# Computing K of four token tiles from raw x at the start, and centring and scaling the kept result later

## The chip, the cores and the metric

The kernel runs on one core of one Trainium2 chip. The metric is the device time of one execution in microseconds (us), the median of several runs; lower is better. Before the change three runs gave 209.97, 210.48 and 213.08 us, median 210.48.

The core has five engines, each with its own instruction stream, synchronised by semaphores: PE (TensorE, matrix multiplication into PSUM), DVE (VectorE), ACT (ScalarE), POOL (GpSimd) and SP (SyncE, which here only issues DMAs). PSUM has 8 banks of 128 x 512 fp32. A DMA is issued by SP or ACT, each of which has a queue of its own, and is carried by 16 DMA engines that both queues share.

## The reference, cut to what matters

`x` is 2048 tokens by D = 640 in bf16. The output is x + A(LN(x)) + B(LN(x)), where LN subtracts the mean of each token and divides by its standard deviation, without learned weights.

```python
def _A_ref(x, wqkv, wo):                 # linear attention, H = 32 heads of 20
    qkv = (x @ wqkv) ...                 # D x 3D: q, k, v
    phi = lambda t: jnp.where(t > 0, t + 1, jnp.exp(t)) + 1e-6
    pq, pk = phi(q), phi(k)
    kv = jnp.einsum("bhsd,bhse->bhde", pk, v)
    z = jnp.einsum("bhsd->bhd", pk)
    num = jnp.einsum("bhqd,bhde->bhqe", pq, kv)
    den = jnp.einsum("bhqd,bhd->bhq", pq, z)[..., None] + 1e-6
    o = num / den
    return ... o ... @ wo
def _B_ref(x, w1, b1, w2, b2):           # dense layer, hidden size F = 1536
    h = _gelu(x @ w1 + b1)
    return h @ w2 + b2
xn = _layernorm(x)
return x + _A_ref(xn, A_wqkv, A_wo) + _B_ref(xn, B_w1, B_b1, B_w2, B_b2)
```

## The kernel before

The 2048 tokens are 16 tiles of P = 128. D is DT = 5 blocks of 128, F is JT = 12 blocks. Everything stays in SBUF: `x_in` (token-major x, later overwritten by `PK` = phi(K)), `xn_tm` (token-major normalised x), `xnT` (feature-major normalised x), `HG` (the gelu output, feature-major), `PQ` (phi(Q), feature-major) and the weights. Every instruction stream is written out by hand: `Pl.ins(engine, ...)` appends to that engine's list, in program order, and adds the waits that its reads and writes need. So an instruction that waits holds up all that stands behind it on its engine, and a DMA that waits on SP holds up the DMAs behind it. PSUM banks are handed out in a ring by `take`.

The stages, in the order of PE:

1. Opening. SP loads x tile by tile, and the four column pieces of W1 between them (`dma_x`, L228; `dma_w1`, L239; piece 0 goes on ACT's queue). PE runs ten filler matmuls on zeros (`filler`, L296). For each tile DVE computes statistics in two halves (`ln_half`, L309, `bn_stats`) and aggregates them (`ln_aggr`, L317), POOL raises the variance to -0.5 (`pow`), and DVE normalises (`ln_norm`, L330). `ln_next(t)` (L422) issues the statistics of tile t + 1, then the normalisation of tile t, then the aggregation of t + 1, in this order on DVE. Tiles 0 to 3 are transposed on PE against an identity matrix and copied from PSUM to `xnT` by DVE or ACT (`transp0`, `transp`, `xnT_copy`); tiles 4 to 15 are transposed by DMA out of `xn_tm` (`dma_start_transpose`, L447, on SP).
2. H. A unit (`h_unit`, L351) is one block of F for n token tiles: five matmuls of n x 128 columns into one bank, and one gelu on ACT from there into `HG`. `units(t0, n, lo, hi)` runs units lo to hi - 1. The first units, for tiles 0 and 1, run as each piece of W1 arrives: 36 units with n = 1, then 30 with n = 2 and 24 with n = 4 (some of n = 2 among the first).
3. K (L471). For each of 16 tiles ten matmuls of 320 columns into a pair of banks; `phi` (L455) is one exp on ACT, one min/add on DVE and one max/add on DVE that reads PSUM and writes `PK` over `x_in`. The K columns of Wqkv are loaded on SP after the DMA transposes.
4. G (L508). For each of five blocks f: 16 tiles times two matmuls accumulate xn^T PK; ACT copies the pair of banks out. Meanwhile DVE sums PK over the tiles in fp32 (`token_sum`, L497) and splits the sum into two bf16 parts (`zhl`); ahead of the last block, PE multiplies them by ones (`z_step`, L486).
5. Q, the small products for the value side (`kvt_step`, `m_step`), the denominators, and the output stage (W2 products and PQ times M into the same banks, 15 tiles and a last one in three parts).

Of the kernel before, what the change touches and what calls it, by code (L numbers as in the profile page):

```python
# [112 lines left out]
def bass_parallel_sum__linear_attn_block__dense_activation_gelu__prompt_kernel(  # L113
# [4 lines left out]
    NT = S // P  # L118
# [18 lines left out]
    with contextlib.ExitStack() as es:  # L137
# [21 lines left out]
        zhl = Mf[:, 2 * D:4 * D].rearrange("p (a d) -> p a d", a=2)  # L159
        b1tmp = sb("b1tmp", [JT, P], BF16)  # L160
# [40 lines left out]
        r_x = [R_("x%d" % t) for t in range(NT)]  # L201
        r_xr = [R_("xr%d" % c) for c in range(NC)]
# [5 lines left out]
        r_Wq, r_Wk, r_Wv, r_W2, r_Wo = R_("Wq"), R_("Wk"), R_("Wv"), R_("W2"), R_("Wo")  # L208
        r_b1tmp, r_b1c, r_b2 = R_("b1tmp"), R_("b1c"), R_("b2")
        r_ident, r_small, r_masks, r_bmask, r_E4, r_warm = R_("ident"), R_("small"), R_("masks"), R_("bmask"), R_("E4"), R_("warm")  # L210
        r_stats = [[R_("stats%d_%d" % (i, h)) for h in range(2)] for i in range(4)]
        r_aggr = [R_("aggr%d" % i) for i in range(4)]
        r_rstd = [R_("rstd%d" % i) for i in range(4)]
# [7 lines left out]
        r_zsum, r_zhl, r_z, r_ZB = R_("zsum"), R_("zhl"), R_("z"), R_("ZB")  # L221
# [11 lines left out]
        def dma_w(eng, dst, src, res):  # L233
            Pl.ins(eng, lambda e: e.dma_start(dst, src), writes=[res], dma=True)  # L234
# [4 lines left out]
        def dma_w1(i, eng="sync"):  # L239
            dma_w(eng, W1[:, :, i * FW:(i + 1) * FW], w1v[:, :, i * FW:(i + 1) * FW], r_W1[i])  # L240
        dma_x(0, 1)
        dma_w("scalar", b1tmp[:], B_b1.rearrange("(a p) -> a p", p=P), r_b1tmp)
        dma_w1(0, "scalar")
        dma_x(1, 1)
        dma_w1(1)
        dma_x(2, 1)
        dma_w1(2)
        dma_x(3, 1)
        dma_w1(3)
        dma_x(4, 2)  # L250
        dma_x(6, 2)
        for c in range(2, NC):
            dma_x(c * CH, CH)
        x_done = len(Pl.records["sync"])
        dma_w("sync", Wqkv[:, :, D:2 * D], wqv[:, :, D:2 * D], r_Wk)
# [10 lines left out]
        Pl.ins(g, lambda e: e.memset(onesb[:], 1.0), writes=[r_small])  # L266
        Pl.ins(g, lambda e: e.memset(ident[:], 0.0), writes=[r_ident])
# [40 lines left out]

        def ln_half(t, h):  # L309
            s = t % 4  # L310
            Pl.ins(v, lambda e: e.bn_stats(stats[:, s, 6 * h:6 * h + 6], x_in[:, t, h * HW:(h + 1) * HW]),  # L311
                   reads=[r_x[t]], writes=[r_stats[s][h]])
            if h == 0:
                Pl.ins(g, lambda e: e.tensor_single_scalar(stats[:, s, 2:3], stats[:, s, 2:3], D * EPS, ALU.add),
                       reads=[r_stats[s][0]], writes=[r_stats[s][0]])

        def ln_aggr(t):  # L317
            s = t % 4
# [11 lines left out]
        def ln_norm(t):  # L330
            s = t % 4
# [32 lines left out]
        CA = 2 * P  # L364
        r_xnA, r_xnB = R_("xn0A"), R_("xn0B")

        def norm0(lo, hi, res):
            Pl.ins(v, lambda e: e.tensor_scalar(xn_tm[:, 0, lo:hi], x_in[:, 0, lo:hi], aggr[:, 0, 0:1], rstd[:, 0:1],
                                                ALU.subtract, ALU.mult),
                   reads=[r_x[0], r_aggr[0], r_rstd[0]], writes=[res, r_xn[0]])  # L370

        def transp0(k0, k1, res):
# [3 lines left out]
                                                          xn_tm[:, 0, k * P:(k + 1) * P], ident[:]))  # L376
                              for k in range(k0, k1)],
                   reads=[res, r_ident], writes=[B_[b]])
            return xnT[:, k0:k1, 0:P], pT[:, 0:(k1 - k0) * P].rearrange("p (k q) -> p k q", k=k1 - k0), b

        def h_first(jbs):
            bs = [take(1) for _ in jbs]
            for (ks, res) in (((0, 1), r_xnTA), ((2, 3, 4), r_xnT[0])):
                for jb, b in zip(jbs, bs):
                    Pl.ins("tensor", [(lambda e, k=k, jb=jb, b=b: e.matmul(  # L385
                        bank(b, 0, P), W1[:, k, jb * P:(jb + 1) * P], xnT[:, k, 0:P],
                        start=(k == 0), stop=(k == DT - 1))) for k in ks],
                        reads=[r_W1[jb * P // FW], res], writes=[B_[b]])
            for jb, b in zip(jbs, bs):
                Pl.ins("scalar", lambda e, jb=jb, b=b: e.activation(  # L390
                    HG[:, jb, 0:P], bank(b, 0, P), ACT.Gelu_apprx_tanh, bias=b1c[:, jb:jb + 1]),
                    reads=[B_[b], r_b1c], writes=[r_HG[0][jb]])

        r_xnTA = R_("xnT0A")
        Pl.ins("scalar", lambda e: e.activation(b1c[:, 0:1], warm[:, 0:1], ACT.Gelu_apprx_tanh),
               reads=[r_warm], writes=[r_b1c])
        filler(10)
        ln_stats(0)
        ln_half(1, 0)
        ln_half(1, 1)  # L400
        ln_aggr(1)
        norm0(0, CA, r_xnA)
        norm0(CA, D, r_xnB)
        dA, sA, bA = transp0(0, 2, r_xnA)
        filler(1)
        dB, sB, bB = transp0(2, DT, r_xnB)
        Pl.ins(v, lambda e: e.tensor_copy(dA, sA), reads=[B_[bA]], writes=[r_xnTA])
        Pl.ins("scalar", lambda e: e.activation(dB, sB, ACT.Copy), reads=[B_[bB]], writes=[r_xnT[0]])
        b1_step()
        ln_norm(1)  # L410
        h_first([0, 1, 2])

        TD = 4
# [16 lines left out]
        xnT_copy(1, transp(1))  # L430
        ln_stats(2)
        ln_next(2)
        units(0, 1, 3, 2 * JQ)
        units(1, 1, 0, 2 * JQ)
        units(0, 2, 2 * JQ, 2 * JQ + 2)
        xnT_copy(2, transp(2))
        units(0, 2, 2 * JQ + 2, JT)
        ln_next(3)
        ln_next(4)
        units(2, 1, 0, JQ)  # L440
        xnT_copy(3, transp(3))
        units(2, 1, JQ, JT)
        units(3, 1, 0, JT)
        for t in range(TD, NT):
            if t > TD:
                ln_next(t)
            Pl.ins("sync", lambda e, t=t: e.dma_start_transpose(xnT[:, :, t * P:(t + 1) * P], xn_tm[:, t, :]),  # L447
                   reads=[r_xn[t]], writes=[r_xnT[t]], dma=True)
        Pl.records["sync"] += late
        run_masks(len(mask_jobs))  # L450
        for (t0, n) in [(4, 2), (6, 2), (8, 4), (12, 4)]:
            units(t0, n, 0, JT)


        def phi(src, b, nb, dst, res_dst, extra_w):  # L455
            s = ring_e[0] % 3
            ring_e[0] += 1
            w = D if nb == 2 else CW
# [3 lines left out]
            br = B_[b:b + nb]  # L462
# [8 lines left out]
        for t in range(NT):  # L471
            b = take(2)
            fns = []
            for k in range(DT):
                for h in range(2):
                    fns.append(lambda e, k=k, h=h, b=b, t=t: e.matmul(  # L476
                        bank(b + h, 0, HW), xnT[:, k, t * P:(t + 1) * P],
                        Wqkv[:, k, D + h * HW:D + (h + 1) * HW], start=(k == 0), stop=(k == DT - 1)))
            Pl.ins("tensor", fns, reads=[r_xnT[t], r_Wk], writes=B_[b:b + 2])
            phi(pair(b), b, 2, PK[:, t, :], r_PK[t], [r_x[t]])  # L480

# [26 lines left out]
        for f in range(DT):  # L508
# [4 lines left out]
            for t in range(NT):  # L513
                Pl.ins("tensor", [(lambda e, t=t, h=h, b=b, f=f: e.matmul(  # L514
# [207 lines left out]
```

## Time and profile before

The profiled execution has a span of 208.6 us; the median of the three runs is 210.48 us, 1.9 us longer. The profile is of one execution, so durations below are of that one.

| engine | busy us | share of the span | instructions |
|---|---|---|---|
| PE matmul | 204.4 | 98% | 1599 |
| PE weight load | 140.6 | 67% | 1599 |
| DVE | 108.1 | 52% | 226 |
| ACT | 74.9 | 36% | 142 |
| POOL | 22.9 | 11% | 62 |

A busy PE is not PE at its peak: matmuls are pipelined and the duration of one contains its latency. What one costs in a dense row is the spacing between starts: the H units of five matmuls of 128 x 512 stand 1.08 us apart, 0.216 us a matmul. The costliest groups are these (busy is the sum, idle is the time the engine stood idle just ahead of them):

| line, engine | what | count | busy us |
|---|---|---|---|
| L355 PE | H units | 435 | 52.0 |
| L622 PE | output, W2 and PQ parts | 510 | 73.9 |
| L476 PE | K | 160 | 21.9 |
| L514 PE | G | 160 | 22.1 |
| L526 PE | Q | 100 | 22.1 |
| L466 DVE | phi, last step, K tiles | 16 | 13.2 |
| L501 DVE | token sum | 14 | 11.6 |

The DMA queues move 17.86 MB in all; 12.62 MB are read from DRAM and 2.62 MB written.

### The profile page before, as it was taken

The page shows a single profiled execution, that of the slowest core. Times are in us where ns is not written, and L with a number is a line of the kernel's source. Part 1 is how long each engine was busy: PE and PEld are TensorE (multiplying, and loading weights), DVE is VectorE, ACT ScalarE, POOL GpSimd, SP SyncE. Part 2 cuts the span into 40 slices and gives each one's busy share as a digit, 9 for nine tenths or more (in the row PEclk, how much of TensorE's full clock was granted, in tenths as well). Part 3 has the DMA queues.
Part 4 walks back from the last instruction along what each step waited for, and adds up shares of the span by engine and source line. Part 5 has one row for each costly group of instructions (what it writes and reads, how often), then busy time and mean ns, then how long its engine had stood idle before and what let it go on. Part 6 is the DMA issues. An engine that isn't in the chain of part 4 may idle for free.

```text
span 208.6 us, 3973 instructions
## 1 busy us (share of the span) xinstructions
PE 204.4 (98%) x1599; PEld 140.6 (67%) x1599; DVE 108.1 (52%) x226; ACT 74.9 (36%) x142; POOL 22.9 (11%) x62
## 2 busy tenths in 40 slices
PE   7999999999999999999999999999999999999995
PEld 2789987444457777777756565577777777777775
DVE  4589970000007888998258965478633422523322
ACT  2689887666676455111153577100000000000000
POOL 3235568300031000000000000000000000000000
PEclk9999999999999999999999999999999999999999
DMA  5998668998000000000000000691110111001001
GB/s 172 348 351 103 104 127 120 376 332 274 3 0 0 0 3 0 0 3 0 0 3 2 0 3 0 198 312 54 63 60 31 61 42 52 31 31 35 31 35 61
DMA packets 22507, 17.86 MB, mean 86 GB/s; under 512 B 9176, under 2 KB 22488, under 8 KB 22488
## 3 DMA queue, kind: packets, MB, share of 16 engines
q1 hardware_dynamic: 21808, 17.11, 28.6%
q10 hardware_dynamic: 680, 0.49, 0.8%
q8 instruction: 12, 0.20, 0.4%
q14 instruction: 7, 0.06, 0.1%
HBM read 12.62 MB, written 2.62 MB: 73 GB/s over the span
## 4 chain that ended last, share of the span: by engine, by line
PE 92%; DVE 4%; DMA 3%; issue 0%; ACTq 0%; DVEq 0%
PE ps L622 33%; PE ps L355 25%; PE ps L514 10%; PE ps L476 10%; PE ps L526 7%; DVE PQ L466 3%; DMA W<-in_B_w_dram 3%; PE ps L658 2%; DVE ek L464 1%; PE ps L535 1%; PE ps L551 1%; PE ps L561 1%; PE ps L385 0%; PE ps L339 0%; ACTq L234 0%
## 5 line engine op out<-in xcount | busy, mean ns | idle before, releaser
L355 PE MATMUL ps<-xnT,W 128*128 128x128 bf16 (+2 forms) x435 | 52.0, 282 | 0.0
L622 PE MATMUL ps<-W,HG 128*128 128x320 bf16 x360 | 51.4, 299 | 0.0
L355 PEld LDWEIGHTS ps<-xnT,W 128*128 128x128 bf16 x435 | 35.5, 98 | 15.8 <-DMA W<-in_B_w_dram 0.2
L622 PEld LDWEIGHTS ps<-W,HG 128*128 128x128 bf16 x360 | 35.1, 98 | 14.2 <-issue 0.4
L359 ACT ACTIVATE HG<-ps,b1c 128x128 bf16<-128x128 f32 (+2 forms) x87 | 40.0, 492 | 12.7 <-PE ps L355 10.6
L464 DVE TENSOR_SCALAR ek<-ek 128x512 bf16<-128x512 bf16 (+1 forms) x36 | 11.1, 307 | 41.7 <-ACT ek L463 40.5
L641 DVE TENSOR_TENSOR out_sb<-ps,xnT 128x640 bf16<-128x640 f32 x15 | 12.4, 825 | 36.2 <-PE ps L622 36.0
L463 ACT ACTIVATE ek<-ps 128x512 bf16<-128x512 f32 (+1 forms) x36 | 23.2, 644 | 19.7 <-PE ps L526 10.1
L622 PE MATMUL ps<-Msb,PQ 128*128 128x320 bf16 x150 | 22.5, 299 | 0.0
L526 PE MATMUL ps<-xnT,Wqkv 128*128 128x512 bf16 x100 | 22.1, 379 | 0.0
L514 PE MATMUL ps<-xPK,xn_tm 128*128 128x320 bf16 x160 | 22.1, 299 | 0.0
L476 PE MATMUL ps<-Wqkv,xnT 128*128 128x320 bf16 x160 | 21.9, 299 | 0.0
L476 PEld LDWEIGHTS ps<-Wqkv,xnT 128*128 128x128 bf16 x160 | 15.7, 98 | 6.2
L514 PEld LDWEIGHTS ps<-xPK,xn_tm 128*128 128x128 bf16 x160 | 15.6, 98 | 6.0
L622 PEld LDWEIGHTS ps<-Msb,PQ 128*128 128x128 bf16 x150 | 14.6, 98 | 5.7
L526 PEld LDWEIGHTS ps<-xnT,Wqkv 128*128 128x128 bf16 x100 | 11.6, 118 | 9.5 <-ACT Msb L556 0.2
L311 DVE BATCH_NORM_STATS2 stats<-xPK 128x6 f32<-128x320 bf16 x32 | 13.6, 466 | 2.9 <-DMA xPK<-in_A_x_dram 2.7
L466 DVE SCALAR_TENSOR_TENSOR PQ<-ps,ek 128x512 bf16<-128x512 f32 x20 | 13.8, 692 | 2.1
L466 DVE SCALAR_TENSOR_TENSOR xPK<-ps,ek 128x640 bf16<-128x640 f32 x16 | 13.2, 825 | 1.7
L501 DVE TENSOR_TENSOR Msb<-Msb,xPK 128x640 f32<-128x640 f32 x14 | 11.6, 825 | 0.5
L518 ACT ACTIVATE W<-ps 128x640 bf16<-128x640 f32 x5 | 3.5, 703 | 18.6 <-PE ps L514 18.6
L321 POOL TENSOR_TENSOR rstd<-aggr,mhalf 128x1 f32<-128x1 f32 x16 | 9.1, 568 | 8.9 <-DVE aggr L319 8.9
(68 smaller groups left out, 93.9 us busy)
## 6 DMA issues: line engine op xcount, KB each, us to landing
xnT<-in_A_x_dram SPq DMA_DIRECT2D x4, 640.0 KB, 6.4
Wqkv<-in_A_wqkv_dram SPq DMA_DIRECT2D x3, 800.0 KB, 7.0
out_dram<-out_sb SPq DMA_DIRECT2D x15, 160.0 KB, 1.8
W<-in_B_w_dram SPq DMA_DIRECT2D x1, 1920.0 KB, 15.2
W<-in_B_w_dram SPq DMA_DIRECT2D x3, 480.0 KB, 7.4
xPK<-in_A_x_dram SPq DMA_DIRECT2D x2, 640.0 KB, 8.5
Wo<-in_A_wo_dram SPq DMA_DIRECT2D x1, 800.0 KB, 10.7
xPK<-in_A_x_dram SPq DMA_DIRECT2D x4, 160.0 KB, 4.4
```

Of the source, the lines that this page charges most:

```text
L311: Pl.ins(v, lambda e: e.bn_stats(stats[:, s, 6 * h:6 * h + 6], x_in[:, t, h * HW:(h + 1) * HW]), reads=[r_x[t]], writes=[r_stats[s][h]])
L355: Pl.ins("tensor", [(lambda e, k=k: e.matmul(bank(b, 0, w), W1[:, k, jb * P:(jb + 1) * P], xnT[:, k, tok], start=(k == 0), stop=(k == DT - ...
L359: Pl.ins("scalar", lambda e: e.activation(HG[:, jb, tok], bank(b, 0, w), ACT.Gelu_apprx_tanh, bias=b1c[:, jb:jb + 1]), reads=[B_[b], r_b1c ...
L463: Pl.ins("scalar", lambda e: e.activation(e2, src, ACT.Exp), reads=br, writes=[r_ek[s]])
L464: Pl.ins(v, lambda e: e.tensor_scalar(et, et, 1.0, 1e-6, ALU.min, ALU.add), reads=[r_ek[s]], writes=[r_ek[s]])
L466: Pl.ins(v, lambda e: e.scalar_tensor_tensor(out=d2, in0=src, scalar=0.0, in1=e2, op0=ALU.max, op1=ALU.add), reads=br + [r_ek[s]], writes= ...
L476: fns.append(lambda e, k=k, h=h, b=b, t=t: e.matmul(bank(b + h, 0, HW), xnT[:, k, t * P:(t + 1) * P], Wqkv[:, k, D + h * HW:D + (h + 1) * ...
L501: Pl.ins(v, lambda e, t=t: e.tensor_tensor(out=zsum, in0=zsum, in1=PK[:, t, :], op=ALU.add), reads=[r_PK[t], r_zsum], writes=[r_zsum])
L514: Pl.ins("tensor", [(lambda e, t=t, h=h, b=b, f=f: e.matmul(bank(b + h, 0, HW), xn_tm[:, t, f * P:(f + 1) * P], PK[:, t, h * HW:(h + 1) * ...
L526: Pl.ins("tensor", [(lambda e, k=k, j=j, b=b: e.matmul(bank(b), Wqkv[:, k, j:D:DT], xnT[:, k, cc], start=(k == 0), stop=(k == DT - 1))) fo ...
L622: return lambda e: e.matmul(bank(b + h, 0, HW), l, r[:, h * HW:(h + 1) * HW], start=(i == 0), stop=(i == JT + DT - 1))
L641: Pl.ins(v, lambda e: e.tensor_tensor(out=halves(out_sb[:, s, :]), in0=pair(b), in1=halves(x_res[:, t, :]), op=ALU.add), reads=B_[b:b + 2] ...
```

## The change

Two things are moved. K of token tiles 0 to 3 is computed at the start, from raw x: tile 0 is transposed on PE from `x_in`, tiles 1 to 3 come transposed by DMA straight out of DRAM (`dma_xT`) into `xTr`, which borrows the part of `HG` that holds tiles 12 to 15 later. The result, not yet centred and scaled, is copied by ACT as fp32 into `Kf`, which borrows `PQ`. Since ((x - m) r) W = r (x W - m c), with c the column sums of W, DVE computes c from the weights (`col_sums`), PE spreads it over the partitions with a matrix of ones, and DVE applies m, c and r to the four kept tiles (`k_center`), in the middle of H. In the K stage PE does twelve tiles; the phi of the four kept ones is put behind tiles 6, 9, 12 and 15, and G takes the tiles in the order 4 to 15, 0 to 3.

The normalised tiles 0 to 3 are no longer transposed on PE but by DMA like the others (`dma_T`). H starts with two tiles at once: 24 units with n = 2 and 36 with n = 4. The K weights are loaded at the start, on ACT's queue, in two pieces of 2 and 3 blocks; W1's pieces 0 and 1 go on ACT's queue behind ACT's copy of tile 0's transpose, pieces 2 and 3 on SP behind the transposes of tiles 0 and 1. x of tiles 8 to 15 is loaded behind the DMA transpose of tile 3. The fillers go from ten and one to five and one. Means and scales of tiles 0 to 3 get slots of their own (`slot`).

```diff
+        csum, cshl = zsum, zhl
+        xTr = HG[:, 0:DT, S - 4 * P:S]
...
+        NR = 4
+        KA = 2
+        def dma_xT(t):
+            Pl.ins("sync", lambda e: e.dma_start_transpose(xTr[:, :, t * P:(t + 1) * P], xv[t * P:(t + 1) * P, :]),
+                   writes=[r_xTr[t]], dma=True)
+
         dma_x(0, 1)
+        dma_w("scalar", Wqkv[:, 0:KA, D:2 * D], wqv[:, 0:KA, D:2 * D], r_WkA)
+        dma_w("scalar", Wqkv[:, KA:DT, D:2 * D], wqv[:, KA:DT, D:2 * D], r_WkB)
         dma_w("scalar", b1tmp[:], B_b1.rearrange("(a p) -> a p", p=P), r_b1tmp)
-        dma_w1(0, "scalar")
+        dma_xT(1)
         dma_x(1, 1)
-        dma_w1(1)
+        dma_xT(2)
+        dma_xT(3)
         dma_x(2, 1)
-        dma_w1(2)
         dma_x(3, 1)
-        dma_w1(3)
-        dma_x(4, 2)
-        dma_x(6, 2)
-        for c in range(2, NC):
-            dma_x(c * CH, CH)
         x_done = len(Pl.records["sync"])
-        dma_w("sync", Wqkv[:, :, D:2 * D], wqv[:, :, D:2 * D], r_Wk)
...
+        def k_mms(b, src, t, ks):
+            return [(lambda e, k=k, h=h: e.matmul(
+                bank(b + h, 0, HW), src[:, k, t * P:(t + 1) * P],
+                Wqkv[:, k, D + h * HW:D + (h + 1) * HW], start=(k == 0), stop=(k == DT - 1)))
+                for k in ks for h in range(2)]
+        def k_raw(t):
+            b = take(2)
+            Pl.ins("tensor", k_mms(b, xTr, t, range(0, KA)), reads=[r_xTr[t] if t else r_xTrA, r_WkA], writes=B_[b:b + 2])
+            Pl.ins("tensor", k_mms(b, xTr, t, range(KA, DT)), reads=[r_xTr[t], r_WkB], writes=B_[b:b + 2])
+            Pl.ins("scalar", lambda e: e.activation(halves(Kf[:, t * D:(t + 1) * D]), pair(b), ACT.Copy),
+                   reads=B_[b:b + 2], writes=[r_Kf[t]])
...
+        def col_sums():
+            Pl.ins(v, lambda e: e.tensor_tensor(out=csum, in0=Wqkv[:, 0, D:2 * D], in1=Wqkv[:, 1, D:2 * D], op=ALU.add),
+                   reads=[r_WkA], writes=[r_csum])
+            for k in range(2, DT):
+                Pl.ins(v, lambda e, k=k: e.tensor_tensor(out=csum, in0=csum, in1=Wqkv[:, k, D:2 * D], op=ALU.add),
+                       reads=[r_WkB, r_csum], writes=[r_csum])
+            Pl.ins(v, lambda e: e.tensor_copy(cshl[:, 0, :], csum), reads=[r_csum], writes=[r_cshl])
+            Pl.ins(v, lambda e: e.tensor_tensor(out=cshl[:, 1, :], in0=csum, in1=cshl[:, 0, :], op=ALU.subtract),
+                   reads=[r_csum, r_cshl], writes=[r_cshl])
+        def k_center():
+            b = take(2)
+            Pl.ins("tensor", [(lambda e, i=i, h=h: e.matmul(bank(b + h, 0, HW), onesf[:], cshl[:, i, h * HW:(h + 1) * HW],
+                                                            start=(i == 0), stop=(i == 1)))
+                              for i in range(2) for h in range(2)],
+                   reads=[r_onesf, r_cshl], writes=B_[b:b + 2])
+            for t in range(NR):
+                kf = Kf[:, t * D:(t + 1) * D]
+                Pl.ins(v, lambda e, kf=kf, t=t: e.scalar_tensor_tensor(
+                    out=halves(kf), in0=pair(b), scalar=aggr[:, t, 0:1], in1=halves(kf), op0=ALU.mult, op1=ALU.subtract),
+                    reads=B_[b:b + 2] + [r_aggr[t], r_Kf[t]], writes=[r_Kf[t]])
+                Pl.ins(v, lambda e, kf=kf, t=t: e.tensor_scalar(kf, kf, rstd[:, t:t + 1], -1.0, ALU.mult, ALU.mult),
+                       reads=[r_rstd[t], r_Kf[t]], writes=[r_Kf[t]])
...
-        xnT_copy(1, transp(1))
+        filler(5)
+        xT0_piece(v, 0, KA, r_xTrA)
+        xT0_piece("scalar", KA, DT, r_xTr[0])
+        dma_w1(0, "scalar")
+        dma_w1(1, "scalar")
+        filler(1)
+        ln_stats(0)
+        ln_half(1, 0)
+        ln_norm(0)
+        ln_half(1, 1)
+        ln_aggr(1)
+        dma_T(0)
+        ln_norm(1)
+        dma_T(1)
+        dma_w1(2)
+        dma_w1(3)
+        dma_x(4, 2)
+        dma_x(6, 2)
+        k_raw(0)
+        k_raw(1)
+        b1_step()
+        k_raw(2)
+        k_raw(3)
         ln_stats(2)
...
+        for t in range(2, NT):
+            ln_next(t)
+            dma_T(t)
+            if t == 3:
+                for c in range(2, NC):
+                    dma_x(c * CH, CH)
         Pl.records["sync"] += late
         run_masks(len(mask_jobs))
-        for (t0, n) in [(4, 2), (6, 2), (8, 4), (12, 4)]:
+        for (t0, n) in [(0, 2), (2, 2), (4, 4)]:
             units(t0, n, 0, JT)
+        units(8, 4, 0, JT // 2)
+        col_sums()
+        k_center()
+        units(8, 4, JT // 2, JT)
+        units(12, 4, 0, JT)
...
-        for t in range(NT):
+        for t in range(NR, NT):
             b = take(2)
...
+            Pl.ins("tensor", k_mms(b, xnT, t, range(DT)), reads=[r_xnT[t], r_WkA, r_WkB], writes=B_[b:b + 2])
             phi(pair(b), b, 2, PK[:, t, :], r_PK[t], [r_x[t]])
+            if t in (6, 9, 12, 15):
+                i = (6, 9, 12, 15).index(t)
+                phi(Kf[:, i * D:(i + 1) * D], i, 0, PK[:, i, :], r_PK[i], [r_x[i]])
...
-            for t in range(NT):
+            for i in range(NT):
+                t = (i + NR) % NT
```

`xT0_piece` is `transp0` and its copy for raw x; `dma_T(t)` is the DMA transpose of L447 as a function. POOL gets one memset more (`onesf`, 128 x 128 ones) ahead of the identity matrix.

## The prediction

> **What bounds the kernel now.** I read the chain of waits first, in order of time.
>
> ```profile
> 1.45 5.47 DMA W<-in_B_w_dram
> ...
> 6.97 1.01 PE ps L385 x15
> ...
> 15.71 44.86 PE ps L355 x345
> 60.57 21.73 PE ps L476 x160
> 82.30 17.39 PE ps L514 x128
> 99.69 0.36 PE ps L488 x10
> ```
>
> Columns: start, duration, what. From 6.97 on PE is the chain almost to the end. So only two things can gain: a start before 6.97, or less PE work. The first 6.97 us are a load, W1's first piece (0.49 MB). From 6.97 to 60.57 the H stage takes 53.6 us.
>
> Second, the page's slices of 5.2 us, for the DMA engines.
>
> ```profile
> PEclk9999999999999999999999999999999999999999
> DMA  5998668998000000000000000691110111001001
> GB/s 172 348 351 103 104 127 120 376 332 274 3 0 0 0 3 0 0 3 0 0 3 2 0 3 0 198 312 54 63 60 31 61 42 52 31 31 35 31 35 61
> ```
>
> The engines are nearly full for the first 15 us with plain loads at 350 GB/s, and then 60 to 90% busy at only 103 to 127 GB/s: there they carry the DMA transposes. PE did not feel the latter, because tiles 0 to 3 were transposed on PE. The window from 22 to 29 us holds transposes alone:
>
> ```profile
> 22.00:29.00 7.00, 7.00 (x67) 6.27 (x65) 6.94 (x22) 5.98 (x13) 4.21 (x12) 1.00 0.73 125
> ```
>
> Last columns: granted clock, DMA share, GB/s. 7.0 us at 125 GB/s are 0.875 MB, 5.3 tiles of 164 kB; 7.0 x 0.73 / 5.3 = 0.96 us of all engines for one transposed tile. A plain tile takes 0.47 us (164 kB at 347 GB/s). For the issue and the landing, the rows of L447:
>
> ```profile
> L447 SPq DMA_TRANSPOSE xnT<-xn_tm x12: 1210/1280/2278, 15.6 to 31.6; - x12
> DMA to landing us min/median/max: 2.6/2.7/4.9
> ```
>
> SP is held 1.28 us (minimum, median and maximum in ns) by each, and each lands 2.7 us after its issue begins.
>
> Third, the timeline of DVE at the end of K:
>
> ```profile
> 84.25 0.81 DVE L498 TENSOR_TENSOR Msb<-xPK 128x640 f32<-128x640 bf16 x1
> 85.09 12.00 DVE L501 TENSOR_TENSOR Msb<-Msb,xPK 128x640 f32<-128x640 f32 x14
> 97.13 0.49 DVE L503 CAST Msb<-Msb 128x640 bf16<-128x640 f32 x1
> 97.66 0.83 DVE L504 TENSOR_TENSOR Msb<-Msb 128x640 bf16<-128x640 f32 x1
> ```
>
> The token sum ends at 98.49; PE asks for it at 99.69. This slack is 1.2 us.
>
> **The sum on PE.** K loses 4 of 16 tiles: 40 matmuls of 21.73 / 160 = 0.136 us, 5.43 us, which come back in the opening. H has 24 units with n = 2 at 0.545 (22 gelus of that size in 11.94 us of the timeline) and 36 with n = 4 at 1.08: 52.0 us, with `k_center`'s four matmuls (0.54) 52.5. That is 1.1 less than before, about the 15 transposes dropped.
>
> **K and G after.** DVE does not get less work: 16 phi, 1.16 us apart when back to back (0.33 + 0.82 and gaps). Its first starts 2.77 us after the K stage (60.57 to 63.34), so the last ends 2.8 + 16 x 1.16 = 21.4 after the start, while PE's 12 tiles take 16.3. No bank holds PE up (four pairs last 5.4 us, the lag is 5.1), but G's first block waits about 1 us for the last kept tile, and token sum follows phi: 14.24 us (84.25 to 98.49), so `z_step` comes 35.7 after the start of K against 39.1 before. Of 5.43 us, 3.4 stay; the rest is a new wait for DVE. From `z_step` to the end nothing changes: 208.65 - 99.69 = 108.96. So the span is the end of H + 35.7 + 109.0. If H ran dense, break-even would be a start of H at 208.65 - 144.7 - 52.5 = 11.5 us.
>
> **The opening after, SP and the DMA engines.** SP issues, in order: x0, xT1, x1, xT2, xT3, x2, x3, T0, T1 (waiting for xn0, xn1), W1 pieces 2 and 3, x4-7, T2, T3 (xn2, xn3), x8-15, T4 and on. ACT issues the K weights in two pieces, and W1's pieces 0 and 1 behind its copy of tile 0's transpose, near 5 us instead of 1.45 for piece 0. A DRAM transpose is nowhere in the trace: between 0.47 (a plain tile) and 1.28 (SP's spacing); I take 0.96, the same operation from SBUF.
>
> Calibration: before, 4.59 MB (x and W1) are 13.2 us at 347 GB/s and the last piece, issued at 8.60, lands 8.9 later, at 17.5: landing = 4.3 + sum. The first H unit needs T1: ahead of it x0-3, K weights and two W1 pieces, 2.46 MB, 7.1 us, and five transposes, 4.8: 16.2. K ends before that, near 13.5 (second K piece near 8, then 5.43).
>
> The first unit with n = 4 needs T7, and this decides. Ahead of it stand all of x, W1 and K weights, 5.41 MB, 15.6 us, and 11 transposes, 10.6: 4.3 + 26.2 = 30.5, if the engines never starve. But they do, by the order: T3 waits on SP for xn3, which on DVE stands behind the statistics of tile 4, and x4 is queued behind T1 and two W1 pieces; x8 stands behind T3, and xn7 behind tile 8's statistics. In time: x4 lands at 4.3 + 10.9 (3.77 MB) + 4.8 = 20.0; statistics and normalising (0.9 + 0.44) make xn3 at 21.4; T3 leaves SP at 22.7; x8 lands 2.4 + 1.4 later (x0's landing, and three tiles more), 26.5; x12 at 28.4, and T4 to T7 behind it at 4 x 0.96: 32.2. Between 30.5 and 32.2 I take 31.4. With plain prices for all transposes the same chain gives x4 at 17.5, xn3 18.9, T3 off SP 20.2, x8 24.0, xn7 25.4, T7 2.7 later at 28.1. With 1.28 each it is 34.0 by the sum and some 1.7 later by the chain.
>
> PE could have been there at 13.5 + 13.1 = 26.6, so it waits some 5 us in three places: for T1, T3 and T7. Then H ends at 31.4 + 38.9 + 0.54 = 70.8, `z_step` is at 106.5, the span 215.5, and with the 1.9 us that the median stands above the span, 217.4.
>
> "TRN2 transpose DMAs are as fast as regular DMAs", says the Trainium skill (Advanced Engine Details and Errata, X-Bar Transpose); 0.96 against 0.47 above disagrees, and by the rule T7 would land near 28 and the time be 214.
>
> **Smaller edits.** Five fillers less: the ten stand 0.435 us apart, against 0.216 for the same shape later, so PE was at half pace for 4.35 us; the shorter row, with waits for K weights behind it, can leave K raw at 0.27 instead of 0.136 a matmul, 0 to 5.4 us more. It is hidden: 13.5 + 5.4 + 13.1 = 32.0, about T7; without that wait up to 5.4 would count. The Trainium skill (TensorE: Matmul & The Clock Gate, Part 1) has the clock released only by some 3.4 us of sustained activity, which speaks against the change; by it K raw would mostly run at half pace.
>
> `col_sums` is 4 x 0.825 + 0.49 + 0.83 = 4.6 us on a DVE that idled from 31 to 63, due 6 units after T11, cover about 4 us. `k_center` holds a pair of banks for up to 5.8 us (four reads of 0.83, three of 0.49 to 0.83 between); the other six banks last 6 x 1.08 = 6.5: nothing, up to 1 us if DVE is late. ACT's four copies (0.70 each) end before the first gelu. POOL's memset (0.2) delays the identity to 1.9, x0 lands at 3.2. The late weights on SP slip by some 12 us; first needed past 100 us.
>
> **Rivals.**
> - Faster or equal: the engines carry transposes beside loads at no cost, T1 lands by 11.5 and nothing waits later. For it: a transpose issued at 15.65 landed in 2.7 us though x12 was still in flight. Against: 0.96, and the chain through xn3 and xn7, which no price removes. At best K starts at 4.1 (x0 at 3.2 and 0.33 MB more): 4.1 + 5.43 + 52.5 + 144.7 = 206.8, time 208.7, -0.9%. It decides from T7 before 24.6 (= 11.5 + 13.1).
> - Cheap transposes, chain kept: T7 at 28.1 (working above) gives 28.1 + 39.4 + 144.7 + 1.9 = 214.1; to 29, 215.
> - Dear DRAM transposes: at 2.5 us each the three add 4.6 us in SP's queue ahead of everything: 222.
>
> **How the numbers follow.** Forecast 0.62, own range 215 to 220; faster or equal 0.12 (208.7 to 211.5); cheap 0.13; dear 0.13. A range of 211.5 to 222 leaves out most of the first rival and the upper half of the last. A measurement of this kernel tells about 2% from no change: below 206.3 needs more than PE's work allows, 0.02 for what I have not seen; 206.3 to 214.7 holds the first rival and most of the cheap case, 0.22; above, 0.76.
>
> **What would show it.** In the changed profile: DMA share near full to about 30 us; PE idle before the first n = 2 and the first n = 4 unit, ended by DMA into xnT, the latter landing at 30 to 33; K's twelve tiles dense, `z_step` 35 to 36 after K's start with PE waiting for DVE ahead of it. Wrong if n = 4 starts before 27, if DRAM transposes take far from 1 us of engines, or if K or H matmuls stand at half pace past 32 us.

## The result, and the profile after

The changed kernel takes 216.67 us (median of four runs, 215.9 to 217.1) against 210.45 us (four runs, 209.97 to 213.08): a ratio of 1.028, 95% interval 1.022 to 1.035. It is slower. The profiled execution took 216.58 us with a span of 214.9 us, 6.3 us above the span of before.

Below, x4 is the load of token tile 4, xn3 the normalised tile 3, and T7 the DMA transpose of the normalised tile 7. The chain of waits of the changed kernel (columns: start, duration, what; only the longest pieces up to the H stage):

```profile
12.64 5.38 DMA xPK<-in_A_x_dram
20.55 4.71 DMA xPK<-in_A_x_dram
26.82 3.67 DMA xnT<-xn_tm
30.95 10.74 PE ps L368 x49
```

Before, one load stood ahead of PE and PE was the chain from 6.97 on. Now three loads and a transpose are 18.2 of the first 31 us of the chain: x1 (4.42 us, not shown), then x4 and 5, then x8 to 11, then T7. Between them stand short pieces of DVE and POOL (statistics, normalisation) and of SP.

The timeline of PE, same kernel (columns: start, duration, group; in brackets the idle time just before it, and what ended it):

```profile
4.52 1.23 PE L382 MATMUL ps<-Wqkv,HG 128*128 128x320 bf16 x4
6.09 2.34 PE L382 MATMUL ps<-Wqkv,HG 128*128 128x320 bf16 x16 [0.34 <-DMA Wqkv<-in_A_wqkv_dram]
...
11.69 1.53 PE L382 MATMUL ps<-Wqkv,HG 128*128 128x320 bf16 x10 [1.70 <-DMA HG<-in_A_x_dram]
14.42 6.71 PE L368 MATMUL ps<-xnT,W 128*128 128x256 bf16 x60 [1.20 <-DMA xnT<-xn_tm]
22.01 6.71 PE L368 MATMUL ps<-xnT,W 128*128 128x256 bf16 x60 [0.88 <-issue]
30.95 19.37 PE L368 MATMUL ps<-xnT,W 128*128 128x512 bf16 x88 [2.23 <-DMA xnT<-xn_tm]
...
70.13 16.46 PE L382 MATMUL ps<-Wqkv,xnT 128*128 128x320 bf16 x120
...
90.45 14.58 PE L549 MATMUL ps<-xPK,xn_tm 128*128 128x320 bf16 x106 [0.72 <-DVE xPK L503]
105.71 0.56 PE L522 MATMUL ps<-onesb,Msb 128*128 128x1 bf16 x10 [0.68 <-DVE Msb L538]
```

The three stalls are there, ahead of the units for tiles 0 and 1 (1.20 us), 2 and 3 (0.88; the trace names no releaser here, in a variant below it names the transpose) and 4 to 7 (2.23): 4.3 us. Ahead of them raw K has waits of its own, the longest 1.70 us for the raw transpose of tile 3 (the row at 11.69). From 30.95 on there is no gap until G, where PE waits for DVE twice: 0.72 us for the phi of tile 15, which on DVE stands behind the phi of three kept tiles, and 0.68 for the token sum.

The timeline of DVE there answers to the one of before:

```profile
90.66 0.82 DVE L503 SCALAR_TENSOR_TENSOR xPK<-PQ,ek 128x640 bf16<-128x640 f32 x1
...
92.26 12.01 DVE L535 TENSOR_TENSOR Msb<-Msb,xPK 128x640 f32<-128x640 f32 x14
...
104.83 0.83 DVE L538 TENSOR_TENSOR Msb<-Msb 128x640 bf16<-128x640 f32 x1
```

The token sum ends at 105.66 and PE takes it at 105.71: the slack of 1.2 us is gone. The product with the ones comes 105.71 - 70.13 = 35.6 us after the start of K. Had the 5.43 us of K been saved in full, it would be 39.1 - 5.43 = 33.7.

So the 6.3 us are accounted for: 4.3 us of stalls ahead of the three groups of units, 1.9 us of waiting for DVE (35.6 - 33.7), and 0.1 us for all else, in which what K and H save is set against the later start. By an estimate from the same rows, K of four tiles at the start would have gained next to nothing even without these waits: K raw ended at 13.2, and with the units of n = 2 behind it (13.1 us) PE would have reached tiles 4 to 7 at 26.3. From there to the end the changed kernel takes 214.9 - 30.95 = 184.0 us, so to end with the kernel before it must be there at 208.65 - 184.0 = 24.65, or at 26.5 without DVE's 1.9 us.

The slices of 5.4 us of the DMA engines' rate, and two windows (columns after the busy times: granted clock, DMA share, GB/s):

```profile
GB/s 203 263 308 207 271 164 129 137 299 376 97 3 0 0 0 0 3 0 3 0 0 2 3 0 3 38 375 102 92 49 40 31 32 85 34 32 31 34 31 61
```

```profile
2.70:14.40 11.70, 8.49 (x50) 4.30 (x48) 4.98 (x14) 4.71 (x8) 2.53 (x7) 1.00 1.14 294
14.40:21.70 7.30, 6.71 (x60) 5.77 (x60) 4.26 (x14) 5.68 (x12) 2.48 (x7) 1.00 0.80 229
```

Nowhere in the opening do the engines reach 350 GB/s as before. The first window has a share above 1, so some time is counted more than once in it, and a share is no clean measure of what capacity is left. In the second one the share is 0.80, and the timeline of SP shows why:

```profile
14.94 5.56 SPq L430 DMA_TRANSPOSE xnT<-xn_tm  x2
20.55 1.13 SPq L234 DMA_DIRECT2D xPK<-in_A_x_dram  x2
```

T2 and T3 hold SP from 14.94 to 20.50, over twice the 2.5 us that two transposes take. T3 waits for xn3, which on DVE stands behind the statistics of tile 4, whose x landed at 18.02. The loads of x8 to 15 stand behind it in SP's queue.

### The profile page after: what moved, and what is told of

Its sections match the earlier page's. It is cut to its first block, busy times and chain, and to the rows that moved or that the text cites. A ratio compares the mean times of both kernels' runs of the same rounds, so it can differ in the third digit from the quotient of the medians.

```text
span 214.9 us, 3618 instructions
## 1 busy us (share of the span) xinstructions
PE 202.9 (94%) x1425; PEld 131.6 (61%) x1433; DVE 115.6 (54%) x236; ACT 72.9 (34%) x116; POOL 24.7 (11%) x63
## 3 DMA queue, kind: packets, MB, share of 16 engines
q1 hardware_dynamic: 25200, 16.95, 28.6%
## 4 chain that ended last, share of the span: by engine, by line
PE 64%; DVE 20%; DMA 8%; issue 2%; SPq 2%; ACT 1%; POOL 0%; DVEq 0%
PE ps L657 32%; PE ps L368 18%; PE ps L561 7%; DMA xPK<-in_A_x_dram 7%; DVE xPK L503 6%; DVE Msb L535 5%; DVE ek L501 3%; DVE PQ L503 3%; PE ps L693 2%; PE ps L549 2%; DMA xnT<-xn_tm 2%; DVE stats L324 1%; PE ps L570 1%; SPq L430 1%; SPq L238 1%
## 5 line engine op out<-in xcount | busy, mean ns | idle before, releaser
L368 PE MATMUL ps<-xnT,W 128*128 128x512 bf16 (+1 forms) x296 | 52.2, 336 | 4.5 <-DMA xnT<-xn_tm 3.4
L368 PEld LDWEIGHTS ps<-xnT,W 128*128 128x128 bf16 x300 | 29.1, 97 | 27.1 <-issue 4.9
L372 ACT ACTIVATE HG<-ps,b1c 128x512 bf16<-128x512 f32 (+1 forms) x60 | 36.1, 602 | 21.0 <-PE ps L368 19.4
L500 ACT ACTIVATE ek<-ps 128x512 bf16<-128x512 f32 (+1 forms) x32 | 20.4, 637 | 15.2 <-PE ps L561 10.1
L501 DVE TENSOR_SCALAR ek<-ek 128x512 bf16<-128x512 bf16 (+1 forms) x36 | 10.9, 304 | 24.5 <-ACT ek L500 24.5
L561 PE MATMUL ps<-xnT,Wqkv 128*128 128x512 bf16 x97 | 21.4, 379 | 0.3 <-issue 0.2
L382 PE MATMUL ps<-Wqkv,xnT 128*128 128x320 bf16 x120 | 16.5, 299 | 0.0
L382 PEld LDWEIGHTS ps<-Wqkv,xnT 128*128 128x128 bf16 x120 | 11.7, 98 | 4.8
L503 DVE SCALAR_TENSOR_TENSOR xPK<-ps,ek 128x640 bf16<-128x640 f32 x12 | 9.9, 824 | 1.3
```

The source lines that it names most:

```text
L368: Pl.ins("tensor", [(lambda e, k=k: e.matmul(bank(b, 0, w), W1[:, k, jb * P:(jb + 1) * P], xnT[:, k, tok], start=(k == 0), stop=(k == DT - ...
L372: Pl.ins("scalar", lambda e: e.activation(HG[:, jb, tok], bank(b, 0, w), ACT.Gelu_apprx_tanh, bias=b1c[:, jb:jb + 1]), reads=[B_[b], r_b1c ...
L382: return [(lambda e, k=k, h=h: e.matmul(bank(b + h, 0, HW), src[:, k, t * P:(t + 1) * P], Wqkv[:, k, D + h * HW:D + (h + 1) * HW], start=( ...
L500: Pl.ins("scalar", lambda e: e.activation(e2, src, ACT.Exp), reads=br, writes=[r_ek[s]])
L501: Pl.ins(v, lambda e: e.tensor_scalar(et, et, 1.0, 1e-6, ALU.min, ALU.add), reads=[r_ek[s]], writes=[r_ek[s]])
L503: Pl.ins(v, lambda e: e.scalar_tensor_tensor(out=d2, in0=src, scalar=0.0, in1=e2, op0=ALU.max, op1=ALU.add), reads=br + [r_ek[s]], writes= ...
```

## The experiments

The theory: PE is late for tiles 4 to 7, partly by an order (T3 behind xn3 behind x4, x8 behind T3), partly by the load that transposes put on SP and the DMA engines, and DVE's lag adds 1.9 us. The rivals: it is the price of a transpose out of DRAM alone; it is the half pace of PE behind fewer fillers; or it is contention that no order removes. One relation helps to read all of them: in the changed kernel the span is the start of the first n = 4 unit + 214.9 - 30.95 = 184.0 us.

**What a transfer costs by itself (`price`).** The kernel before, with four plain loads, four transposes out of DRAM and four out of SBUF put on SP in the K and G stages, when the DMA engines are otherwise idle, into parts of `PQ` that are overwritten later:

```diff
+        gate = probe(["plain"] * 4, [r_PK[2]])
+        gate = probe(["dram"] * 4, gate)
+        gate = probe(["sbuf"] * 4, gate)
```

> The kernel before, with twelve extra DMAs of one token tile each, issued by SP in the K and G stages when the DMA engines are idle: four plain loads of x, then four transposes of x out of DRAM, then four transposes of xn out of SBUF, each group after the last one landed, into a part of PQ that is not yet in use. Capacity theory (the DMA engines' time decides): a plain tile takes about 0.47 us of all engines, a transposed one about 0.96, from DRAM as from SBUF, and stands 1.28 us behind the one ahead. Rival (dear DRAM transposes): 1.5 to 2.5 us each from DRAM. Rival (as cheap as a plain tile): 0.5. The span should stay at 208.6 within 0.5.

It took 210.53 us beside 210.63. Three windows, one for each kind:

```profile
67.00:71.30 4.30, 4.30 (x34) 3.11 (x32) 3.74 (x8) 2.11 (x3) 0.00 (x0) 1.00 0.52 152
71.30:79.50 8.20, 8.20 (x63) 5.89 (x61) 6.96 (x13) 4.23 (x6) 0.00 (x0) 1.00 0.59 82
79.50:87.00 7.50, 7.50 (x58) 5.41 (x56) 6.68 (x11) 2.23 (x4) 0.00 (x0) 1.00 0.44 87
```

Length times share over four: a plain tile 4.30 x 0.52 / 4 = 0.56 us of all engines, a transpose out of DRAM 8.20 x 0.59 / 4 = 1.21, one out of SBUF 7.50 x 0.44 / 4 = 0.83. The DRAM case holds a disturbance, seen in the rows of its line:

```profile
L494 SPq DMA_TRANSPOSE PQ<-in_A_x_dram x4: 1206/1278/2301, 71.4 to 75.3; - x4
...
DMA to landing us min/median/max: 2.8/3.5/4.5
```

One of the four issues held SP 2.3 us instead of 1.28, and two of the four landed after 4.2 and 4.5 us; the others took 2.8 and 2.9, hardly more than the 2.6 to 2.7 out of SBUF. So a transpose out of DRAM is not the 2.5 us of the dear rival, and by this measure neither kind is as cheap as a plain tile.

**The order alone (`order37`).** Tiles 3 and 7 are normalised ahead of the statistics of the next tile; nothing else changes:

```diff
         def ln_next(t):
+            if t in (3, 7):
+                ln_norm(t)
             if t + 1 < NT:
                 ln_half(t + 1, 0)
                 ln_half(t + 1, 1)
-            ln_norm(t)
+            if t not in (3, 7):
+                ln_norm(t)
```

> The changed kernel, with one thing in another order on DVE: tiles 3 and 7 are normalised ahead of the statistics of tiles 4 and 8, not behind them. No byte less moves. Order theory (T3 waits on SP for xn3, behind it x8 to x15, and xn7 stands behind tile 8's statistics): T3 leaves SP near 17 instead of 21.7, the first unit with n = 4 starts at 27.5 to 28.5 instead of 30.95, the span falls by 2.5 to 3.5 us to about 212. Capacity theory: x12 and the transposes need the same engine time, the unit starts at 30 to 31 and the span falls by less than 1 us.

214.26 us (213.81 to 214.66) against 210.63: ratio 1.016 (1.010 to 1.022), span 212.6. SP and PE:

```profile
15.08 2.53 SPq L430 DMA_TRANSPOSE xnT<-xn_tm  x2
```

```profile
21.94 26.14 PE L368 MATMUL ps<-xnT,W 128*128 128x256 bf16 x150 [0.70 <-DMA xnT<-xn_tm]
```

T2 and T3 now leave SP dense, x8 is issued at 17.66 instead of 20.55, and the last stall is gone: the units with n = 4 follow in one piece (at about 28.5; 212.6 - 184.0 gives 28.6). The other two stalls are nearly as they were (1.24 and 0.70). So 2.3 us of the 6.3 were the order of the two normalisations on DVE; how they divide between tile 3 and tile 7 this run doesn't tell, as it moves both. The stalls for T1 and T3 have another cause: T3 was issued at 16.4 here and at 19.3 in the changed kernel, and landed at 21.8 and 21.9, so its landing did not follow its issue.

**Raw tiles transposed on PE (`peraw`).** Tiles 1 to 3 of raw x are transposed on PE and copied by ACT, so no transpose reads DRAM:

```diff
-        dma_xT(1)
         dma_x(1, 1)
-        dma_xT(2)
-        dma_xT(3)
         dma_x(2, 1)
...
+        raw_T(1)
         k_raw(0)
+        raw_T(2)
         k_raw(1)
+        raw_T(3)
```

> The changed kernel, with raw x of tiles 1 to 3 transposed on PE (15 transposes, about 1 us) and copied by ACT, instead of by DMA out of DRAM; the rest as in the change. Capacity theory: three transposes less, 2.9 us, so the first unit with n = 4 starts near 28 and the span is 212 to 213. Order theory: x1 to x3 land about 3 us earlier, so xn1, T1, W1's last pieces and x4 follow some 2 us earlier, and the unit starts at 28 to 29.5, span 212.5 to 213.5; the two theories are told apart only by what ends the waits: here SP's wait for xn3 should again stand ahead of x8. Rival (the DRAM transposes cost nothing): 214.5 to 215.

215.27 us (214.99 to 215.66), ratio 1.021 (1.016 to 1.026), span 213.5.

```profile
12.54 6.71 PE L365 MATMUL ps<-xnT,W 128*128 128x256 bf16 x60
20.89 6.71 PE L365 MATMUL ps<-xnT,W 128*128 128x256 bf16 x60 [1.64 <-issue]
```

```profile
12.25 7.18 SPq L438 DMA_TRANSPOSE xnT<-xn_tm  x2
```

The first stall is gone (T1 is there at least 1.9 us earlier), but PE only comes sooner to the next two: T3 waits on SP for xn3 as before, 7.18 us instead of 5.56. Of 1.9 us, 1.5 arrive at the n = 4 units, which begin at 29.41. Whether the transposes out of DRAM cost this by their time on SP or by that on the DMA engines, this run doesn't separate.

**Normalised tiles transposed on PE (`pexn`).** Tiles 0 to 3 of xn go back to PE, with the copies on DVE, and x8 to 15 are issued directly behind x6:

```diff
-        dma_T(0)
         ln_norm(1)
-        dma_T(1)
...
+        for c in range(2, NC):
+            dma_x(c * CH, CH)
...
+        xnT_copy(0, transp(0))
+        xnT_copy(1, transp(1))
...
+        ln_next(2)
+        units(0, 2, 0, 8)
+        xnT_copy(2, transp(2))
+        ln_next(3)
+        units(0, 2, 8, 11)
+        xnT_copy(3, transp(3))
+        units(0, 2, 11, JT)
```

> The changed kernel, with xn of tiles 0 to 3 transposed on PE and copied by DVE as before the change, no longer by DMA; so no DMA on SP waits for xn0 to xn3, and x8 to x15 are issued behind x6. K from raw x stays. PE gets 20 transposes (about 1.3 us). Both theories expect T7 earlier: by the sum of engine time 4.3 + 15.6 + 7 x 0.96 = 26.6. PE is then the limit: K to 13.2, 13.1 of units and the transposes, first unit with n = 4 at 27 to 28.5, span 211 to 212.5. If neither holds, 214 to 215.

It missed: 217.21 us (215.25 to 217.88), ratio 1.029 (1.022 to 1.035); the profiled execution is the fastest, 215.25 us with a span of 213.5, at a granted clock of 1.00, where the records of the other three show 0.992. Two lines show why:

```profile
6.33 4.26 PE L382 MATMUL ps<-Wqkv,HG 128*128 128x320 bf16 x16 [0.44 <-DMA Wqkv<-in_A_wqkv_dram]
```

```profile
18.77 0.49 DVE L360 COPY xnT<-ps 128x640 bf16<-128x640 bf16 x1 [2.97 <-PE ps L352]
```

First, raw K stood at half pace here, 4.26 / 16 = 0.27 us a matmul, until 10.6, where the changed kernel had 0.146 from 6.09 on. Second, I had put DVE's copy of tile 2 ahead of the statistics of tile 4, and it waited 2.97 us for a transpose that PE reached at 18.3. T4 was issued only at 22.6, and the n = 4 units began at 29.42. So this run tells nothing for or against the theory; it made a new wait in place of the old one.

**Both on PE (`peboth2`).** Raw tiles 1 to 3 and xn tiles 0 to 3 on PE, with the transposes of tiles 0 and 1 ahead of the third raw tile, and those of 2 and 3 behind two units, so that no copy holds up DVE:

```diff
+        ln_stats(2)
+        bt = [transp(0), transp(1)]
+        xnT_copy(0, bt[0])
+        xnT_copy(1, bt[1])
+        ln_half(3, 0)
+        ln_half(3, 1)
+        ln_norm(2)
+        ln_aggr(3)
         k_raw(2)
         k_raw(3)
...
+        units(0, 2, 0, 2)
+        xnT_copy(2, transp(2))
+        xnT_copy(3, transp(3))
+        ln_stats(4)
+        units(0, 2, 2, JT)
```

> The changed kernel with no DMA transpose for tiles 0 to 3: raw x of tiles 1 to 3 and xn of tiles 0 to 3 are transposed on PE (35 transposes, about 2 us), K from raw x stays; all loads are issued one behind the other, and tile 3 is normalised ahead of tile 4's statistics. Both theories: the transposes and loads are out of PE's way, K ends near 12.5 with 0.6 of transposes between, units with n = 2 run dense, the first unit with n = 4 starts at 26.5 to 27.5, and by start + 184.0 (the same distance in the three runs so far) the span is 210.5 to 211.5. With the clock at half pace during K raw, as in the run with xn on PE, 2 us more. If something else holds H: 213 and more.

214.09 us (213.86 to 214.35), ratio 1.015 (1.009 to 1.020), span 212.4: less than hoped for. Its chain of waits is mostly one transfer:

```profile
4.73 12.01 DMA W<-in_B_w_dram
```

It ends where PE resumes the units, at 16.79, after a stall of 1.34 us. W1's pieces 0 and 1 are on ACT's queue behind ACT's copy, while SP's queue now holds all of x; piece 1 took 12.0 us to land, where the changed kernel's median for the two was 6.4.

**W1 ahead (`peboth3`).** Piece 0 goes on ACT's queue right behind the K weights, pieces 1 to 3 on SP ahead of x4:

```diff
         dma_w("scalar", Wqkv[:, KA:DT, D:2 * D], wqv[:, KA:DT, D:2 * D], r_WkB)
+        dma_w1(0, "scalar")
...
-        dma_w1(0, "scalar")
-        dma_w1(1, "scalar")
         filler(1)
...
+        dma_w1(1)
         dma_w1(2)
```

> As the run with no DMA transposes for tiles 0 to 3, with the W1 pieces issued at once: piece 0 on ACT's queue behind the K weights, pieces 1 to 3 on SP behind x0 to x3 (in that run piece 1, on ACT's queue, landed at 16.7 and held PE); tile 0's first K matmuls stand ahead of tile 1's transposes. Both theories: units run dense from the end of K near 12.7, the first unit with n = 4 starts at 26.2 to 27, by start + 184.0 the span is 210.2 to 211. If K raw runs at half pace: 212 to 213.

212.88 us (212.8 to 213.02) against 210.30: ratio 1.012 (1.011 to 1.014), span 211.1. No stall is left behind 13.38:

```profile
13.38 1.25 PE L366 MATMUL ps<-xnT,W 128*128 128x256 bf16 x10
...
15.03 31.60 PE L366 MATMUL ps<-xnT,W 128*128 128x256 bf16 x198
```

The n = 4 units begin at 211.1 - 184.0 = 27.1, 3.9 us before those of the changed kernel. That is the part of the loss that sits in the opening.

**DVE's lag: without the kept phi (`nophi`), with it early (`ephi`), with `z_step` late (`zlate`).** `nophi` leaves the phi of the four kept tiles out, so that G and the token sum read raw x there:

```diff
-            if t in (6, 9, 12, 15):
-                i = (6, 9, 12, 15).index(t)
-                phi(Kf[:, i * D:(i + 1) * D], i, 0, PK[:, i, :], r_PK[i], [r_x[i]])
```

`ephi` takes the same lines out and computes it in the middle of H, ahead of the last 12 units:

```diff
         units(8, 4, JT // 2, JT)
+        for i in range(NR):
+            phi(Kf[:, i * D:(i + 1) * D], i, 0, PK[:, i, :], r_PK[i], [r_x[i]])
         units(12, 4, 0, JT)
```

`zlate` puts the product with the ones behind G's last block:

```diff
-            if f == DT - 1:
-                z_step()
...
+        z_step()
```

> The changed kernel without phi of the four kept tiles (four exp, eight DVE operations); G and the token sum read raw x in their place. DVE theory: K's twelve tiles keep DVE under PE, G starts without a wait and the sum is there before PE asks; the ones-product stands 33.7 us after the start of K instead of 35.6, the span falls by 1.9 to 213.0. Rival (PE is held up by banks or by something else after K): no more than 0.5 us.

> The changed kernel, with phi of the four kept tiles in the H stage, ahead of the last twelve units, when DVE is idle; ACT changes its table twice more (1.28 us each) and runs four exp of 0.7 there. DVE theory: the ones-product comes 33.7 us after the start of K, worth 1.9; ACT's pause of 5.4 us is covered by the banks but for 0 to 1.5 us at the end of H. Span 213.0 to 214.5. If the pause isn't covered: 215 to 217.

> The changed kernel, with the token sum's product (z_step) behind the last block of G instead of ahead of it, so that PE doesn't wait for the split sum there. DVE theory (after K, PE waits about 1 us for the last kept phi and about 1 us for the sum): the wait of 0.7 us ahead of the ones-product goes, G's own start still waits, the span is 213.9 to 214.3. If DVE's lag passes on into Q instead: 214.9.

`nophi` took 214.61 us (one execution, span 212.9), `ephi` 215.51 us (215.09 to 217.09; ratio 1.023, 1.015 to 1.031; span 213.9), `zlate` 216.07 us (215.59 to 217.6; ratio 1.025, 1.018 to 1.032; span 213.8). Their openings differ from one execution to the next (n = 4 units at 30.69, 31.66 and 30.55), so I compare what lies behind: 182.2, 182.2 and 183.2 us instead of 184.0. PE in `nophi`, whose K began at 70.08:

```profile
86.38 17.55 PE L546 MATMUL ps<-xPK,xn_tm 128*128 128x320 bf16 x128
103.76 0.53 PE L519 MATMUL ps<-onesb,Msb 128*128 128x1 bf16 x10
```

G is dense, and the product with the ones comes 33.7 us after the start of K: all 5.43 us are kept. In `ephi` it is the same row of 17.55 us, and the product comes at 104.73, also 33.7 us after a K that began at 71.05. So DVE's lag costs 1.8 us, of which the wait for the token sum is 0.8 (`zlate`) and the rest G's first block. Done early, phi is free, though ACT stops its gelus from 59.0 to 64.4 for two table loads (1.28 us each) and four exps: the banks of PSUM covered it, and the PE row of H shows no gap there.

**All together (`best3`), and a last try (`best4`).** `best3` is `peboth3` with the early phi of `ephi` and with the first three additions of the token sum in H too:

```diff
             phi(Kf[:, i * D:(i + 1) * D], i, 0, PK[:, i, :], r_PK[i], [r_x[i]])
+        Pl.ins(v, lambda e: e.tensor_tensor(out=zsum, in0=PK[:, 0, :], in1=PK[:, 1, :], op=ALU.add),
+               reads=[r_PK[0], r_PK[1]], writes=[r_zsum])
+        for t in range(2, NR):
+            Pl.ins(v, lambda e, t=t: e.tensor_tensor(out=zsum, in0=zsum, in1=PK[:, t, :], op=ALU.add),
+                   reads=[r_PK[t], r_zsum], writes=[r_zsum])
         units(12, 4, 0, JT)
```

`best4` adds two moves against the waits that were left, for the K weights and for b1:

```diff
-        dma_w("scalar", Wqkv[:, KA:DT, D:2 * D], wqv[:, KA:DT, D:2 * D], r_WkB)
+        dma_w("scalar", Wqkv[:, KA:DT - 1, D:2 * D], wqv[:, KA:DT - 1, D:2 * D], r_WkB)
...
         dma_x(1, 1)
+        dma_w("sync", Wqkv[:, DT - 1:DT, D:2 * D], wqv[:, DT - 1:DT, D:2 * D], r_WkC)
...
-        b1_step()
...
         k_raw(3)
+        b1_step()
```

> That kernel, with phi of the four kept tiles and their part of the token sum in the H stage. By the sum: 1.9 less, from the wait of G and of the ones-product (the run with the early phi showed 33.7 instead of 35.6 between K's start and the ones-product): span 208.2 to 209.2, the same as before the change within 0.3%. If it is below 207.5, K at the start does gain once its transposes and its phi are out of the way; if above 210, something is still unseen.

> The version before this one (all transposes of tiles 0 to 3 on PE, early phi) with two waits of PE in its opening taken away: the bias transpose, which waited 0.6 us for b1 at 9.4, stands behind the fourth raw K, and the last block of the K weights is loaded on SP's queue behind x1, so that the second K group starts at 6.1 instead of 6.5. Units start 0.8 to 1.0 us earlier: span 208.2 to 208.5, time 210.0 to 210.3, ratio to before 0.998 to 1.001. If it is at 1.003 or above again, the waits only moved; below 0.997 it would beat both kernels.

`best3`: 211.02 us (six runs, 210.91 to 211.43) against 210.30, ratio 1.0035 (1.0023 to 1.0046), span 209.2. `best4`: 211.24 us (twelve runs) against 210.29, ratio 1.0033 (1.0018 to 1.0047), span 209.5. PE in `best3`:

```profile
6.53 0.97 PE L380 MATMUL ps<-Wqkv,HG 128*128 128x320 bf16 x6 [0.49 <-DMA Wqkv<-in_A_wqkv_dram]
...
10.01 0.18 PE L311 MATMUL ps<-ident,b1tmp 12*128 12x12 bf16 x1 [0.59 <-DMA b1tmp<-in_B_b_dram]
...
13.40 1.26 PE L366 MATMUL ps<-xnT,W 128*128 128x256 bf16 x10
...
66.46 16.46 PE L380 MATMUL ps<-Wqkv,xnT 128*128 128x320 bf16 x120
```

The start of K in the kernel before, by the same timeline (the chain writes 60.57, the end of the last H matmul):

```profile
60.41 21.90 PE L476 MATMUL ps<-Wqkv,xnT 128*128 128x320 bf16 x160
```

H starts at 13.40 instead of 6.97, 6.43 us later; it is 0.38 shorter (53.06 to K's start, against 53.44), and from the start of K to the end there are 142.7 us instead of 148.2, 5.5 less: 6.43 - 0.38 - 5.5 = 0.55, the difference of the spans. With the stalls behind raw K and DVE's lag removed, the change is no gain but a loss of 0.3%. Two waits of 0.49 and 0.59 us are left ahead of H; without them, by subtraction, it would take 209.9 us, still within 0.2% of the kernel before. In `best4` the waits only moved, to 0.67 us for the K weights and 0.82 us for the x that PE transposes.

**The fillers (`fill10`).** The changed kernel with ten fillers instead of five.

```diff
-        filler(5)
+        filler(10)
```

> The changed kernel with ten fillers at the start again instead of five. Order and capacity theories: the clock of K raw doesn't matter, T1, T3 and T7 decide; tile 0's transpose and K raw start 2 us later and still end before T1 is used; W1's piece 0 is issued 2 us later and still lands in time: span 214.6 to 215.4. Clock theory (the shorter row of fillers costs time): 213.5 or less.

217.18 us (one execution), span 215.4:

```profile
6.45 2.96 PE L382 MATMUL ps<-Wqkv,HG 128*128 128x320 bf16 x20
...
31.52 3.83 PE L368 MATMUL ps<-xnT,W 128*128 128x512 bf16 x17 [2.11 <-DMA xnT<-xn_tm]
```

Raw K is at full pace from its first matmul and ends at 12.3 instead of 13.2, and the n = 4 units are no earlier: they wait for T7 as before. PE's pace in the opening is hidden, so that rival falls.

## Why the prediction held, point by point

- **Direction and size.** Forecast 217.4 us, 215 to 220 for the likeliest case; measured 216.67. The mechanism was the one described: three stalls, and a wait for DVE in place of part of what K saves. The 1.9 us added to the span were 1.7 (216.58 - 214.9); the 1.9 set a median beside the span of another execution. The DMA share, forecast near full to about 30 us, was 60 to 90% by slices up to 32 us.
- **K and G.** `z_step` 35.7 us after the start of K: 35.6. From there to the end 109.0: 109.2. Both waits are in the rows, and `nophi` and `ephi` show that they are DVE's. The one at G's first block was forecast for the last kept tile and is for tile 15, whose phi stands behind those of three kept tiles; the cause is the same.
- **The end of raw K.** Taken near 13.5, measured 13.2, but by another wait: the second piece of the K weights was there by 6.09 instead of near 8, and the raw transpose of tile 3, for which no wait was forecast, held PE for 1.70 us.
- **The first n = 4 unit.** Taken at 31.4, measured 30.95, but by terms that were off in both directions. x4 was to land at 20.0 and landed at 18.02 (2.0 early); from there to x8 6.5 us were forecast and 7.2 passed (18.02 to 25.25); from x8 to the first n = 4 unit 5.7 were forecast and 5.7 passed. The chain of 32.2 thus became 30.95, and the mean taken with the 30.5 of the sum hid the error. That the last leg agrees is luck as well: the forecast had T4 to T7 follow x12 at 0.96 us each, but T4 to T6 landed from 27.7 to 28.8, close behind x12 (27.1), and T7 came last at 30.5 because it was issued only at 26.8, when xn7, behind tile 8's statistics, was done (26.5) and T6 had left SP.
- **The step that was mis-sized** is "landing = 4.3 + sum" with 0.96 for each transpose. T1 landed at 14.2 instead of at 16.2, and x4 is early by about as much; the same five transposes stand ahead of both. With the 4.3 kept, x4 gives (18.02 - 4.3 - 10.9) / 5 = 0.56 us a transpose, no more than `price` gave for a plain tile (0.56), while `price` gives 0.83 and 1.21 for the transposes by themselves. Either a start term taken from plain loads alone is too long, or transposes beside plain loads use time that a share counts more than once (the share of 1.14). The runs don't tell these apart. In the flooded first 14 us the cheap rival's price was thus nearer, and its x4 (17.5) too; it failed behind that, where the order counts and not the price: x8 was to land at 24.0 and T7 at 28.1.
- **The order.** That T3 waits on SP for xn3, behind tile 4's statistics, and x8 behind T3, was read from the instruction order and was right; `order37` puts 2.3 us on this together with the place of xn7 behind tile 8's statistics.
- **The page on transposes.** "TRN2 transpose DMAs are as fast as regular DMAs" (the Trainium skill, Advanced Engine Details and Errata, X-Bar Transpose) would have given 214. Alone, they took 0.83 to 1.21 us of the engines against 0.56, and SP 1.28 us each against 0.34 to 0.43 for a plain tile of the same size; in the flooded opening, if the 4.3 is kept, the landings agree with the page better than with my 0.96.
- **The clock.** "0 to 5.4 us more, hidden": nearly 0 here, as only the first four matmuls of raw K stood at half pace; `fill10` shows that it is hidden, and `pexn` that it can be paid: half pace until 10.6, 9.3 us after PE's first work at 1.25, with no gap over 0.44 us between. The 3.4 us of sustained activity in the Trainium skill (TensorE: Matmul & The Clock Gate, Part 1) is exceeded in all three: full pace came between 5.75 and 6.09 in the changed kernel, and with ten fillers, dense from 1.25, not before 5.6.
- **Costs taken as nothing.** `col_sums`, `k_center` and ACT's copies show no wait of PE; the one row of `k_center` on PE took 0.54 us, as forecast. The late weights on SP slipped by some 5 us (W2 issued at 42.09 instead of 36.94), not 12.
- **The best case** of the first rival, 208.7, was out of reach of the version with the stalls and the lag removed (`best3`, 211.02), as PE came to the first units only at 13.40 there: raw K and 30 transposes lie ahead of them, with 1.1 us of waits.

Left open: what makes T1 and T3 land late with all transfers in flight (that T3's landing did not follow its issue speaks for the shared DMA engines, but no run isolates it), why single transposes hold SP some 2.1 to 2.5 us and land late, and what sets the moment at which PE comes to full pace from one execution to the next. No version was found that beats the kernel before.

## What to carry to other kernels

Before moving work into an idle stretch at the start, write down the time at which each of its operands can be there, and what stands behind it in each queue: here the 2.4 us between the first raw K matmul (4.52) and the old start of H (6.97) could not hold 5.43 us of K, and the transfers that it needed stood ahead of others that PE had never waited for. When work leaves one engine in a stage, look for who was second there (DVE's token sum was there only 1.2 us before PE asked for it, and a gain of 5.4 was cut to 3.5). A waiting transpose on a queue of loads holds up the loads behind it: here the order of two lines on another engine, for which T3 and T7 waited, was worth 2.3 us.

## What the runs showed of the hardware

- The same 164 kB tile took 0.56 us of all DMA engines as a plain load, 0.83 transposed out of SBUF and 1.21 transposed out of DRAM (with one disturbance in it), by share times length; a transpose held SP 1.28 us in the median, which by an estimate lets one queue of transposes move some 128 GB/s.
- With SP's queue full of x, the second of two pieces of 0.49 MB on ACT's queue took 12.0 us to land (`peboth2`).
- PE code that is the same as far as the third raw tile was at full pace from 6.1 us in the profiled execution of the changed kernel and from 10.6 in that of `pexn`, at a granted clock of 1.00 in the records of both.
